# Loading k by head without regrouping, and moving one regrouping of q behind a sum

## The chip, the cores and the metric

One NeuronCore of a Trainium2 chip runs the whole program. The metric is the device time of one execution in microseconds (us), on the slowest core, which here is the only one. A run is compared with runs of the kernel before on the same chip. Runs of the kernel in its undisturbed state are called fast.

## The reference, cut to what matters

Attention without a softmax, a norm per head, then a gated feed-forward layer with a sigmoid-gated residual:

```python
kv  = einsum('bhsd,bhse->bhde', k, v)          # batch 8, heads 8, seq 576, head_dim 64
out = einsum('bhsd,bhde->bhse', q, kv)
x   = out / sqrt(mean(out*out, -1) + 1e-6) * g_norm      # then (4608, 512)
...
ffn = (gelu(x @ w_gate) * (x @ w_val)) @ w_out           # d_ff 1536
y   = x + sigmoid(x @ w_res) * ffn
```

The inputs and outputs are fp32; the kernel works in fp16 with fp32 sums.

## The kernel before

The work goes by blocks of 512 tokens, one for each batch, with the last 64 tokens of every batch gathered in a ninth. While TensorE (PE) does the feed-forward products of block b, the attention of batch b + 1 is slipped in between. The load of a batch brings q and k in by head; VectorE (DVE) regroups both by token. The load of k by head writes the layout `[P, H, NJ*D]`; the regrouped tile has `[P, NJ, H, D]` (P: 128 partitions, H: 8 heads, NJ: 4 tokens in each partition, D: the head's 64 elements).

```python
raw[b, "q"] = stage.tile([P, H, NJ * D], FP16, tag="qraw", name="qraw")
raw[b, "k"] = stage.tile([P, H, NJ * D], FP16, tag="kraw", name="kraw")
nc.gpsimd.dma_start(out=raw[b, "q"], in_=rows4(q, b, 0, H))
nc.gpsimd.dma_start(out=raw[b, "k"], in_=rows4(k, b, 0, H))
...
def by_token(b, which):
    nc.vector.tensor_copy(
        out=b16_t[b, which].rearrange("p j h d -> p h j d"),
        in_=raw[b, which].rearrange("p h (j d) -> p h j d", j=NJ))
...
# a_kv: 32 products per batch read k (8 more read the last tokens)
lhsT=k16[:, j, h, :] if j < NJ else kl[:, h, :]
```

A block ends with its output product, done as seven half-size products over sums of its operands. The order on PE is A, D, A, E, A, F, A; VectorE's sum `wF` has to be done between the second A and the third, because the third overwrites what it reads:

```python
def others():                                            # cut
    prod(w["A"], s_[1], wo_t[:, 1], False)               # PE
    sub(nc.vector, w["F"], w["A"], w["d"], ALU.add)      # VectorE: the sum wF
    prod(w["E"], a_of(blk, 1, 2), b_of(2, 1), False)
    pf((0, 0), w["E"])                                   # VectorE: the gate on wE
    prod(w["A"], s_[2], wo_t[:, 2], False)               # overwrites wA: waits for the sum
    c22 = res_all[part((1, 1))]
    sub(nc.vector, c22, w["A"], w["d"], ALU.add)         # VectorE: the next sum
    prod(w["F"], s_[3], b_of(2, 2), False)
```

The regroupings for batch b are queued on VectorE near the end of block b - 2, so batch 3's stand at the end of block 1, in front of that block's sum wF. Behind q's regrouping SyncE issues the DMA transpose that makes qT.

## Time and profile before

| | |
|---|---|
| time, first three runs | 344.58, 345.43, 344.43 us |
| PE busy | 331.9 us of a 345.4 us span |
| PE's wait on the sum wF, block 1 | 1.2 us, the longest behind the opening |
| regroupings of k on VectorE | 7, mean 738 ns |

The prediction below shows the lines. The rule for reading them: busy shares say which engine is nearest its limit (PE), but what a change gives is decided by PE's waits, each with its releaser, so the list of PE's waits comes first and the order of time around the one wait comes second. In the order of time a line holds the start in us, the duration, the engine, the source line, the operation, output and inputs, the count, and in brackets the idle time before it with its releaser. PEld is PE's loading of weights, ACT is ScalarE, POOL is GpSimd, SPq is SyncE's DMA queue. In a line of the list of waits the numbers are us in total, times, and the longest in us.

### The profile page before, as it was taken

The numbers are of one execution on the slowest core, as the hardware profiler recorded it, in microseconds if no ns is written. First come the engines' busy times: TensorE is split into PE (matmuls) and PEld (weight loads), VectorE is DVE, ScalarE is ACT, GpSimd is POOL, SyncE is SP. The second block draws the span as 40 slices with busy tenths as digits, with TensorE's granted clock in tenths as the row PEclk, the third lists the DMA queues.
The fourth block names the chain that finished last, engine by engine and source line by source line (L and its number), as shares of the span: only waits on it lengthen the run. The fifth ranks groups of instructions, "written<-read, shape, count | busy, mean of one in ns | idle before, by whom it ended". The sixth has DMA issues, their size and how long they took to land.

```text
span 345.4 us, 6165 instructions
## 1 busy us (share of the span) xinstructions
PE 331.9 (96%) x2432; PEld 188.0 (54%) x2432; DVE 236.5 (68%) x446; ACT 150.1 (43%) x265; POOL 103.1 (30%) x121
## 2 busy tenths in 40 slices
PE   8789999999899999999999999999999999999992
PEld 3544454445744475447544764476447644764481
DVE  5665549769859987698578976885688735453643
ACT  3573384274336352535263615361736133623350
POOL 2692161980064108200820083005000600050013
PEclk9899999999999999999999999999999999999997
DMA  7999999669589263966395439744003120030004
GB/s 244 290 178 204 195 204 166 168 95 150 117 108 164 94 123 120 165 60 128 130 167 43 102 114 174 79 92 153 17 0 61 63 76 2 1 121 4 0 2 121
DMA packets 76399, 38.81 MB, mean 112 GB/s; under 512 B 42066, under 2 KB 73810, under 8 KB 76370
## 3 DMA queue, kind: packets, MB, share of 16 engines
q0 software_dynamic: 38752, 17.17, 40.1%
q1 hardware_dynamic: 37184, 20.71, 21.6%
q10 hardware_dynamic: 434, 0.52, 0.5%
q8 instruction: 19, 0.31, 0.4%
q14 instruction: 10, 0.08, 0.1%
HBM read 38.80 MB, written 9.44 MB: 140 GB/s over the span
## 4 chain that ended last, share of the span: by engine, by line
PE 69%; DVE 2%; issue 0%; POOL 0%; POOLq 0%; DVEq 0%
PE gps L336 21%; PE vps L336 20%; PE wA L431 10%; PE rps L356 6%; PE wF L431 3%; PE wD L431 2%; PE w L431 2%; PE wE L431 2%; PE kvp L187 1%; PE op L205 1%; DVE t L282 1%; DVE hid L325 1%; DVE hid_s L404 0%; DVE t L296 0%; POOL osb L526 0%
## 5 line engine op out<-in xcount | busy, mean ns | idle before, releaser
L324 ACT ACTIVATE ge<-gps 128x512 f16<-128x512 f32 x108 | 64.3, 597 | 133.1 <-PE gps L336 127.8
L325 DVE TENSOR_TENSOR hid<-ge,vps 128x512 f16<-128x512 f16 x108 | 73.8, 684 | 63.2 <-PE vps L336 60.8
L336 PE MATMUL vps<-xT,wv 128*128 128x512 f16 x424 | 108.8, 379 | 0.4 <-DVE hid L325 0.4
L336 PE MATMUL gps<-xT,wg 128*128 128x512 f16 x424 | 109.0, 379 | 0.0
L470 POOL TENSOR_TENSOR osb<-osb,t 128x512 f32<-128x512 f32 x28 | 36.1, 1309 | 155.6 <-DVE osb L466 148.6
L336 PEld LDWEIGHTS <-wv 128*128 128x128 f16 x424 | 41.5, 98 | 50.6 <-issue 0.7
L336 PEld LDWEIGHTS <-wg 128*128 128x128 f16 x424 | 40.2, 98 | 45.4 <-issue 0.4
L431 PEld LDWEIGHTS <-hid_s 128*128 128x128 f16 x384 | 37.5, 98 | 6.3 <-issue 1.4
L356 PE MATMUL rps<-wr,xT 128*128 128x512 f16 x144 | 32.7, 379 | 0.0
L431 PEld LDWEIGHTS <-hid 128*128 128x128 f16 x288 | 28.2, 98 | 5.1
L365 ACT ACTIVATE th<-rps 128x512 f32<-128x512 f32 x36 | 21.5, 597 | 19.0 <-PE rps L356 19.0
L356 PEld LDWEIGHTS <-xT 128*128 128x128 f16 x144 | 14.1, 98 | 16.8
L224 DVE TENSOR_REDUCE ss<-sq 128x8 f32<-128x512 f32 x32 | 20.6, 679 | 2.9 <-ACT sq L222 2.7
L431 PE MATMUL wA<-wo_ts,hid_s 128*128 128x256 f16 x168 | 20.6, 273 | 1.2 <-DVE wF L404 1.2
L370 ACT ACTIVATE th<-th 128x512 f32<-128x512 f32 x36 | 19.9, 622 | 0.0
L282 DVE TENSOR_TENSOR t<-op,ny 128x512 f16<-128x512 f32 x28 | 17.9, 682 | 0.1
L222 ACT ACTIVATE sq<-op 128x512 f32<-128x512 f32 x28 | 15.3, 597 | 4.5 <-PE op L205 4.2
L296 DVE TENSOR_TENSOR t<-t,g 128x512 f16<-128x512 f16 x36 | 16.2, 498 | 0.1
L404 DVE TENSOR_TENSOR hid_s<-hid 128x1536 f16<-128x1536 f16 x16 | 15.3, 955 | 0.3
L526 POOL TENSOR_TENSOR osb<-osb,t 128x512 f32<-128x512 f32 (+1 forms) x4 | 4.3, 1078 | 27.8 <-DVE osb L522 27.8
L373 PE MATMUL fps<-wo,hid 128*128 128x512 f16 x48 | 11.2, 379 | 0.0
L431 PE MATMUL wD<-wo_ts,hid_s 128*128 128x256 f16 x84 | 10.3, 273 | 0.1
(133 smaller groups left out, 326.5 us busy)
## 6 DMA issues: line engine op xcount, KB each, us to landing
out_dram<-osb SPq DMA_DIRECT2D x14, 512.0 KB, 2.6
qraw<-in_q_dram POOLq DMA_DIRECT2D x7, 512.0 KB, 8.2
kraw<-in_k_dram POOLq DMA_DIRECT2D x7, 512.0 KB, 9.9
v<-in_v_dram POOLq DMA_DIRECT2D x7, 512.0 KB, 11.9
out_dram<-osb SPq DMA_DIRECT2D x5, 256.0 KB, 2.8
wg<-in_moe_w_gate_dram POOLq DMA_DIRECT2D x2, 512.0 KB, 9.2
wv<-in_moe_w_val_dram POOLq DMA_DIRECT2D x2, 512.0 KB, 9.4
wo<-in_moe_w_out_dram POOLq DMA_DIRECT2D x2, 512.0 KB, 14.2
```

The source lines that it names most:

```text
L222: nc.scalar.activation(out=sq, in_=src, func=AF.Square)
L224: nc.vector.tensor_reduce(out=out_, in_=sq, op=ALU.add, axis=mybir.AxisListType.X)
L282: nc.vector.tensor_tensor(out=t, in0=o, in1=scale, op=ALU.mult)
L296: nc.vector.tensor_tensor(out=t_t[blk][:, jj, :], in0=t_t[blk][:, jj, :], in1=g16, op=ALU.mult)
L324: nc.scalar.activation(out=ge, in_=gps, func=AF.Gelu)
L325: nc.vector.tensor_tensor(out=hids[blk][:, f, :], in0=ge, in1=vps, op=ALU.mult)
L336: nc.tensor.matmul(ps[:, j0 * P : j1 * P], lhsT=w[:, cc, :], rhs=xT_t[blk][:, j0:j1, cc, :], start=(cc == 0 and j0 == 0), stop=(cc == NP - ...
L356: nc.tensor.matmul(rps, lhsT=xT_t[blk][:, j, cc, :], rhs=wr16[:, cc, :], start=(cc == 0), stop=(cc == NP - 1),)
L365: nc.scalar.activation(out=th, in_=rps, func=AF.Tanh, scale=0.5)
L370: nc.scalar.activation(out=th, in_=th, func=AF.Copy, scale=0.5, bias=0.5)
L431: nc.tensor.matmul(ps[:, e - es[0], :], lhsT=a[:, f, e * P : (e + 1) * P], rhs=b[:, f, :], start=(start and e == es[0] and f == 0), stop=( ...
L470: nc.gpsimd.tensor_tensor(out=res_all[of], in0=res_all[of], in1=t_t[blk][of], op=ALU.add)
```

## The change

The intent: let the products read k in the layout in which it is loaded, so that VectorE need not regroup it, and keep batch 3's regrouping of q from standing in front of block 1's sum.

```diff
-        b16_t[b, "k"] = qkvp.tile([P, NJ, H, D], FP16, tag="k16", name="k16")
+        by_head = [P, H, NJ * D] if b > 0 else [P, NJ, H, D]
+        b16_t[b, "k"] = qkvp.tile(by_head, FP16, tag="k16", name="k16")
-        raw[b, "k"] = stage.tile([P, H, NJ * D], FP16, tag="kraw", name="kraw")
-        nc.gpsimd.dma_start(out=raw[b, "k"], in_=rows4(k, b, 0, H))
+        nc.gpsimd.dma_start(out=b16_t[b, "k"], in_=rows4(k, b, 0, H))
...
-                        lhsT=k16[:, j, h, :] if j < NJ else kl[:, h, :],
+                        lhsT=k16[:, h, j * D : (j + 1) * D] if j < NJ else kl[:, h, :],
...
             pf((0, 0), w["E"])
+            for f in rest:
+                f()
             prod(w["A"], s_[2], wo_t[:, 2], False)
...
-            at(m - 1, NF, lambda: by_token(b, "q"))
-            at(m - 1, NF + 1, lambda: by_token(b, "k"), *begin)
+            if b == 3:
+                amid_out[m - 1] = [lambda: by_token(b), *begin]
+            else:
+                at(m - 1, NF, lambda: by_token(b))
+                at(m - 1, NF + 1, *begin)
```

Cut: the staging of the first columns of the value weight, which used k's staging tile and now uses one of k's two tiles, and the places for batches 1 and 2, which lose their k line in the same way.

More of the change, by code (lines that the diff above doesn't have):

```diff
@@ L104, in load_batch, with by_token @@
             load_qr(i)
-    def by_token(b, which):
+    def by_token(b):
         nc.vector.tensor_copy(
-            out=b16_t[b, which].rearrange("p j h d -> p h j d"),
-            in_=raw[b, which].rearrange("p h (j d) -> p h j d", j=NJ),
+            out=b16_t[b, "q"].rearrange("p j h d -> p h j d"),
+            in_=raw[b, "q"].rearrange("p h (j d) -> p h j d", j=NJ),
         )
@@ L438, in prod, with out_by_products @@
                 )
-    def out_by_products(blk, later):
+    def out_by_products(blk, later, rest=()):
         w = {}
@@ L632 @@
     for n, t in (("g", moe_w_gate), ("v", moe_w_val)):
-        r = "q" if n == "g" else "k"
-        w_raw[n] = stage.tile([P, H, NJ * D], FP16, tag=r + "raw", name=f"w{n}f")
+        pool, tag = (stage, "qraw") if n == "g" else (qkvp, "k16")
+        w_raw[n] = pool.tile([P, H, NJ * D], FP16, tag=tag, name=f"w{n}f")
         w_raw[n] = w_raw[n].rearrange("p a b -> p (a b)").bitcast(FP32).rearrange("p (c f) -> p c f", c=NP)
@@ L864, in attn_plan_1 @@
         plan = {
-            NF - 1: [lambda: by_token(b, "q")],
-            NF: [lambda: by_token(b, "k")],
+            NF - 1: [lambda: by_token(b)],
             NF + 3: [
@@ L883 @@
     plans = [{} for _ in range(B + 1)]
+    amid_out = {}
     hold = consts.tile([1, 1], FP16, name="hold")
@@ L905, in plan_attn @@
         if b == 2:
-            at(m, 0, lambda: by_token(b, "q"))
-            at(m, 1, lambda: by_token(b, "k"), *begin)
+            at(m, 0, lambda: by_token(b))
+            at(m, 1, *begin)
             k0, o0, n0 = 4, 6, 9
         else:
-            at(m - 1, NF, lambda: by_token(b, "q"))
-            at(m - 1, NF + 1, lambda: by_token(b, "k"), *begin)
+            if b == 3:
[3 more added lines that the diff above has]
+                at(m - 1, NF + 1, *begin)
             k0, o0, n0 = 1, 3, 7
@@ L955, in products @@
                 s_rest(blk)
-                outs.extend(out_by_products(blk, blk == 1) if blk < B else out_last(blk))
+                outs.extend(out_by_products(blk, blk == 1, amid_out.get(blk, ())) if blk < B else out_last(blk))
             plan.setdefault(NF - 1, []).append(products)
```

## The prediction

> **What bounds the kernel now.** I read the busy row first, then who TensorE (PE) waited for, then VectorE (DVE) and PE in order of time where the one wait lies that the change can touch.
>
> ```profile
> PE 331.9 (96%) x2432; PEld 188.0 (54%) x2432; DVE 236.5 (68%) x446; ACT 150.1 (43%) x265; POOL 103.1 (30%) x121
> ```
>
> PE is busy for 331.9 of 345.4 us. About 13.5 us are all that better feeding could give, and most of that is the opening and the last stores. VectorE at 68% is not the bound as an average, so work taken off it pays only where PE is waiting for it. The list of what PE waited for:
>
> ```profile
> PE kvp L718 <- DVE v L689: 2.5, 2, 2.3
> PE wA L431 <- DVE wF L404: 1.2, 1, 1.2
> ...
> PE vps L336 <- DVE hid L325: 0.4, 1, 0.4
> ```
>
> The first is the opening, before the changed code. The second is one wait of 1.2 us: an output product (wA) waits for a sum on VectorE (wF). The third is a wait for the gated hidden tile. The stretches of 1 us show where the second lies (columns after the stretch: PE, PEld, DVE, ACT, POOL busy, clock, DMA):
>
> ```profile
> 84.00:90.00 6.00, 6.00 (x53) 4.99 (x51) 5.93 (x10) 4.22 (x8) 0.00 (x0) 1.00 0.29 21
> 90.00:91.00 1.00, 0.13 (x2) 0.00 (x0) 1.00 (x3) 0.22 (x1) 0.00 (x0) 1.00 0.27 56
> 91.00:92.00 1.00, 0.65 (x6) 0.58 (x6) 0.89 (x2) 0.00 (x0) 0.00 (x0) 1.00 1.12 214
> ```
>
> PE is full up to 90, then nearly empty for 1.2 us while DVE is full. This is the end of block 1, the products of its output. DVE in order of time there:
>
> ```profile
> 88.06 1.42 DVE L296 TENSOR_TENSOR t<-t,g 128x512 f16<-128x512 f16 x4
> 89.40 0.69 DVE L107 COPY q<-qraw 128x2048 f16<-128x2048 f16 x1
> 90.01 0.69 DVE L107 COPY k<-kraw 128x2048 f16<-128x2048 f16 x1
> 90.61 0.69 DVE L404 TENSOR_TENSOR wF<-wA,wd 128x512 f32<-128x512 f32 x1
> 91.21 0.68 DVE L466 TENSOR_TENSOR osb<-th,wE 128x512 f32<-128x512 f32 x1
> 92.92 0.69 DVE L404 TENSOR_TENSOR osb<-wA,wd 128x512 f32<-128x512 f32 x1 [1.03 <-issue]
> ```
>
> and PE:
>
> ```profile
> 88.66 1.47 PE L431 MATMUL wE<-wo,hid 128*128 128x256 f16 x12
> 91.35 1.47 PE L431 MATMUL wA<-wo_ts,hid_s 128*128 128x256 f16 x12 [1.22 <-DVE wF L404]
> 92.66 1.47 PE L431 MATMUL wF<-wo,hid_s 128*128 128x256 f16 x12
> 93.97 1.47 PE L431 MATMUL wA<-wo_ts,hid 128*128 128x256 f16 x12
> 95.28 1.03 PE L336 MATMUL gps<-xT,wg 128*128 128x512 f16 x4
> ```
>
> The reader is to see that both regroupings of batch 3 (q, then k) stand in VectorE's queue directly ahead of the sum wF, and that PE's next product of wA starts 0.05 us after that sum ends (90.61 + 0.69 = 91.30, then 91.35). VectorE has no idle time in front of the copies: it reaches the sum late because of its queue, not its data. Unhindered, twelve matmuls start 1.31 us apart (92.66 to 93.97), so this product was due at 88.66 + 1.31 = 89.97; PE loses 1.38 us from start to start, recorded as 1.22.
>
> **What the Trainium skill says.** "VectorE: DVE Perf Modes", section "The perf-mode tier table", gives a 16-bit copy of 2048 elements in SBUF 693 ns; the regroupings here take 685 to 687 ns in the median. The same page's section on the errata gives an fp32 tensor_tensor of 512 elements 691 ns; the sums here take 690. So either copy costs the queue what the sum itself costs. "The DRAIN you can't avoid" describes a start-to-start gap after each operation; here starts lie 0.60 to 0.61 us apart, less than the 0.69 us durations, and I count with 0.61. "DMA: Bandwidth & Descriptors", section "Latency and other measured facts", gives DMA transposes 261 GB/s in one kernel; here 214 GB/s moved between 91 and 92 us, so I use the trace's own 4.4 us from issue to landing.
>
> **The change part by part.**
>
> 1. k is loaded straight into the tile that the products read; the regrouping is gone for batches 1 to 7. That takes seven copies off VectorE, 7 x 0.738 = 5.2 us of busy time. PE reads k by columns of 64 elements of one head in either layout, so its 40 instructions per batch stay: no cost, no gain. Six of the seven copies lie where PE has no recorded wait: the copies at 42.73, 63.44 and from batch 4 on. I checked batch 4, the closest call: copies at 125.49 and 126.10, sum at 126.70 ending 127.39, and PE goes on at 127.59 with no idle time. Value of these six: 0. The batch 3 copy, at 90.01, is worth 0.61 us of the sum's start.
>
> 2. Batch 3's regrouping of q goes from before the sum to behind the next operation (the gate that reads wE). That takes a second 0.61 us from ahead of the sum. Together the sum starts at 89.40, where the four scalings of t let go of VectorE, and ends at 90.09; PE goes on at 90.09 + 0.05 = 90.14 in place of 91.35. Gain 1.21 us; 0.17 us of the 1.38 stays, because the scalings are still in front.
>
> 3. What the moved copy costs at its new place. The gate on wE needs that product's end (88.66 + 1.47 = 90.13) and ScalarE's sigmoid (ends 90.22), so it starts near 90.25. The copy follows near 90.85 and ends near 91.55. The next sum waits for PE's wA, started at 90.14: before, it began 92.92 - 91.35 = 1.57 after that start, so it is due at 91.71. The copy fits into idle time that was there already (1.03 us in front of that sum). Cost 0. If it came 0.2 us late, the product that overwrites wA, which is due at 90.14 + 2.62 = 92.76, would still find the sum finished near 92.6.
>
> 4. Buffers. The staged gate weight now borrows one of k's two tiles. k of batch 1 then goes where batch 0's k was; those products start at 17.57 and take 0.4 us, and the load is issued at 22.85. k of batch 2 goes over the staged weight, whose last cast ends near 19.1, and is issued at 43.98. Later loads follow the key-value product of two batches earlier by a whole block. The loads arrive in time: 22.85 + 16.8 (the longest) = 39.7 against a first use at 45.7; 43.98 + 12.7 = 56.7 against 67.4; 73.10 + 8.5 = 81.6 against about 97.6. Cost 0.
>
> Sum: -0.61 - 0.61 + 0 = -1.2 us, 344.58 - 1.2 = 343.4 us, or 0.35%. Everything behind 91 us should shift earlier as a block, since PE is full there.
>
> **The rivals.**
>
> A. The next block's input takes the place of the wait. Block 2's first product reads xT, whose DMA transpose is issued at 89.52, behind the scalings and so not moved by the change:
>
> ```profile
> 89.52 1.78 SPq L313 DMA_TRANSPOSE xT<-t  x1
> 91.46 2.25 SPq L300 DMA_TRANSPOSE qT<-q  x1
> ```
>
> It lands 4.4 us later, at 93.92. PE will want it at 95.28 - 1.21 = 94.07. That leaves 0.15 us, about what passes between a transpose's landing and the instruction that waits for it (qT: 91.46 + 4.3 = 95.76, seen by GpSimd at 95.93). For it: the margin is nothing; against it: it is not negative, and behind it the transposes of q are not earlier than before. I expect 0 to 0.1 us back; a landing 0.5 us later would make it 343.9.
>
> B. The later qT becomes the bound. q is regrouped near 91.55 rather than 90.09, but its transpose had to wait for SyncE's issue of xT until 91.46 anyway, so it starts near 91.65. Landing at 96 and PE's use at 103.5 - 1.2 = 102.3 leave 6 us. GpSimd's loads for batch 4 sit behind it (97.03) and move by 0.2 us; k is due 27 us later. Worth 0.
>
> C. Less VectorE work helps wider, for instance the wait in block 2 for the hidden tile. There PE's starts 116.25 and 117.72 are 1.47 apart in place of 0.86, and wD starts 0.3 late at 123.65. For it: VectorE is full from 111 to 124. Against: no k copy lies there, and the backlog comes from operations that move with PE. If it vanished anyway, the time would be 342.5.
>
> D. The two copies of batch 2 beside GpSimd's sums (1.66 and 1.04 us) show contention. "SBUF - State Buffer", section "Who interferes with whom", says that copies in two-port mode exclude GpSimd for their whole length, and the reverse. Removing one may end GpSimd's sums up to 1 us sooner, but PE waits for neither: VectorE is idle again by 65.1. Worth 0.
>
> **Range and chances.** The three times before spread over 1.0 us, nearly the gain. The size rests on one read interval, so I allow 0.5 us back (A) and as much more (C): 343.4 us, 8 in 10 within 342.7 to 344.2. A change of 2% is 6.9 us, six times the gain and half of all PE idle time: faster 0.01, within 2% 0.98, slower 0.01.
>
> **What would show it.** In the profile after: no copy of k on VectorE after the opening, VectorE busy about 231 us; the sum wF of block 1 directly behind the scalings, ending near 90.1; PE's wait on it 0.2 us or gone; q's copy behind the gate, with little idle time after it; block 2's first gate product near 94.1, not held. It would be wrong if PE waits there for xT (rival A), if the sum is still late because something else slid ahead of it, if a key-value product waits for k's transfer, or if PE's total is shorter elsewhere than at 90 us.

(Where the text says that the staged gate weight borrows k's tile, it is the value weight; the argument about the tile is the same.)

## The result, and the profile after

Ratios are the mean time of one kernel's fast runs over that of the other's fast runs of the same rounds, so they are not quite the ratio of the medians quoted. The square brackets hold a 95% interval. All differences below are under 1%.

| | median | runs | ratio to before |
|---|---|---|---|
| before, at first | 344.50 us | 4 | |
| after, at first | 344.04 us (342.86 to 344.98) | 4 | 0.9981 [0.9956, 1.0006] |
| before, beside e1 to e4 | 344.42 us (344.08 to 344.96) | 11 | |
| after, repeated (e2) | 343.26 us (342.96 to 343.87) | 5 | 0.9973 [0.9960, 0.9986] |

The busy row of the changed kernel:

```profile
PE 330.8 (97%) x2432; PEld 186.8 (55%) x2432; DVE 231.8 (68%) x439; ACT 150.2 (44%) x265; POOL 102.3 (30%) x121
```

VectorE has seven instructions and 4.7 us less; PE has the same instructions. What PE waited for:

```profile
PE kvp L720 <- DVE v L691: 1.4, 1, 1.4
...
PE vps L336 <- DVE hid L325: 0.4, 1, 0.4
```

No wait on wF is left, and the wait in block 2 for the hidden tile is as before. VectorE in order of time at the end of block 1:

```profile
86.51 1.42 DVE L296 TENSOR_TENSOR t<-t,g 128x512 f16<-128x512 f16 x4
87.85 0.69 DVE L404 TENSOR_TENSOR wF<-wA,wd 128x512 f32<-128x512 f32 x1
88.76 0.69 DVE L466 TENSOR_TENSOR osb<-th,wE 128x512 f32<-128x512 f32 x1 [0.22 <-ACT th L370]
89.36 0.69 DVE L107 COPY q<-qraw 128x2048 f16<-128x2048 f16 x1
90.15 0.69 DVE L404 TENSOR_TENSOR osb<-wA,wd 128x512 f32<-128x512 f32 x1
```

and PE:

```profile
87.09 1.47 PE L431 MATMUL wE<-wo,hid 128*128 128x256 f16 x12
88.59 1.47 PE L431 MATMUL wA<-wo_ts,hid_s 128*128 128x256 f16 x12
89.90 1.47 PE L431 MATMUL wF<-wo,hid_s 128*128 128x256 f16 x12
91.21 1.47 PE L431 MATMUL wA<-wo_ts,hid 128*128 128x256 f16 x12
92.52 1.03 PE L336 MATMUL gps<-xT,wg 128*128 128x512 f16 x4
```

The sum stands directly behind the scalings of t, the copy of q behind the gate, and the third A starts 1.50 us after E where it was 2.69 before (88.66 to 91.35). That is 1.19 us. But the two profiled spans differ by 2.8 us (345.4 and 342.6). The other 1.6 us is there before the changed code begins: block 0's first full gate product starts here before,

```profile
23.98 1.03 PE L336 MATMUL gps<-xT,wg 128*128 128x512 f16 x4
```

and here after:

```profile
22.42 1.03 PE L336 MATMUL gps<-xT,wg 128*128 128x512 f16 x4
```

So I measured two distances that leave the opening out. D1 goes from that start to block 2's first gate product; D2 goes from there to the start of the last group of twelve output products. Before: D1 = 95.28 - 23.98 = 71.30 us, D2 = 337.21 - 95.28 = 241.93 us. After: D1 = 92.52 - 22.42 = 70.10 us, D2 = 334.46 - 92.52 = 241.94 us. The change is worth 1.20 us, all of it in D1; nothing is given back later.

### The profile page after: what moved, and what is told of

It reads as the page before. It is cut to its first block, busy times and chain, and to the rows that moved or that the text cites. A ratio compares the mean times of both kernels' runs of the same rounds, so it can differ in the third digit from the quotient of the medians.

```text
span 342.6 us, 6156 instructions
## 1 busy us (share of the span) xinstructions
PE 330.8 (97%) x2432; PEld 186.8 (55%) x2432; DVE 231.8 (68%) x439; ACT 150.2 (44%) x265; POOL 102.3 (30%) x121
## 4 chain that ended last, share of the span: by engine, by line
PE 90%; DVE 4%; DMA 2%; POOL 1%; SPq 1%; issue 1%; POOLq 0%; DVEq 0%
PE gps L336 27%; PE vps L336 26%; PE wA L431 10%; PE rps L356 8%; PE fps L373 3%; PE wD L431 3%; PE wE L431 3%; PE wF L431 3%; PE w L431 2%; DMA kf<-in_k_dram 2%; PE kvp L187 2%; PE op L205 1%; DVE t L282 1%; DVE t L759 1%; DVE hid L325 1%
```

## The experiments

The theory: PE waits in block 1 because two copies stand in VectorE's queue ahead of the sum; each is worth 0.6 us, and the other copies are worth nothing. The rivals: VectorE's total load matters; only one part of the change matters; the opening is changed too; the gain is near a new bound.

**e1, e2: the two kernels once more.** No edit.

> The kernel before, unchanged, timed against itself. My theory: the change is worth 1.2 us at the end of block 1 and the rest of the difference between two runs is made in the first 24 us, where transfers land at varying times. Then this run's ratio is 1.000 with single times about 1 us apart, and its profile has, as before, 71.30 us from block 0's first full gate product (23.98) to block 2's first (95.28), whatever the opening took. Rival (the two kernels' openings differ by something in the change): every run of the kernel before opens late, with its first full gate product near 24.0 us as in the first profile, and none near 22.4.

> The changed kernel, unchanged, for a tighter interval. My theory: 1.2 us of 344.5, a ratio of 0.9965 give or take 0.001, and 70.10 us from block 0's first full gate product to block 2's first, as in its first profile (22.42 to 92.52). Rival (opening differs too): 2.8 us less, ratio 0.992, as the two profiled runs alone would have it. Other rival (the gain is given back later): ratio 0.999 to 1.000.

Measured: e1 344.33 us, ratio 1.0010 [0.9984, 1.0037], five runs at 344.12 to 344.48 and one at 347.46. Its D1 is 71.29 us, but its opening ended at 21.02, 3.0 us earlier than in the first profile of the same kernel.

e2 came to 343.26 us, ratio 0.9973, D1 70.10 us, opening ended at 21.00. So the rival of a changed opening falls: the same program opened at 23.98 and at 21.02, and the two programs at 21.02 and 21.00. The opening is later where the first load of v lands later: its landing took 7.3 us in the first profile of before, 5.4 in e1, 6.3 after, 5.4 in e2 and 7.6 in e3 (opening ended at 25.75). The landing is not all of it. PE's first product of v starts at 10.65 in the first profile of before and at 8.81 in e1, 1.84 us apart; the other 1.1 us came behind it. PE had waited 2.35 us for v there, and the granted clock then fell, which it did not do in e1 (columns: PE, PEld, DVE, ACT, POOL busy, then the clock, DMA share, GB/s):

```profile
11.00:12.00 1.00, 1.00 (x13) 1.00 (x11) 0.29 (x1) 0.59 (x1) 0.27 (x1) 0.50 1.06 367
```

With a spread of this size in the total, four runs could show 0.46 us for a change of 1.2; eleven against five runs show 344.42 - 343.26 = 1.16 us.

**e3: the load of k alone.** q's regrouping stays ahead of the sum.

```diff
-            if b == 3:
+            if b == 99:        # q of batch 3 keeps its old place
                 amid_out[m - 1] = [lambda: by_token(b), *begin]
```

> k is loaded by head without regrouping, but batch 3's regrouping of q stays in front of the sum. My theory: the sum starts one copy (0.61 us) earlier than before, so PE's wait between two products at the end of block 1 goes from 1.38 us (start to start, over 1.31) to 0.77, and the distance from block 0's first full gate product to block 2's first is 70.7 us; ratio 0.998. Rival (only the place of q's copy matters, since the sum waits for the queue to reach it behind q): 71.3 us, ratio 1.000.

Measured: 344.25 us, ratio 1.0010 [0.9975, 1.0045]. One of the six runs, the profiled one, is at 348.29 with a late opening; the others lie at 343.58 to 344.46, so the timing cannot carry a verdict on 0.6 us. The trace can: D1 = 96.45 - 25.75 = 70.70 us, as expected to the last digit, and one copy is left ahead of the sum:

```profile
91.17 0.69 DVE L107 COPY q<-qraw 128x2048 f16<-128x2048 f16 x1
91.78 0.69 DVE L404 TENSOR_TENSOR wF<-wA,wd 128x512 f32<-128x512 f32 x1
```

and PE waits half as long:

```profile
92.53 1.47 PE L431 MATMUL wA<-wo_ts,hid_s 128*128 128x256 f16 x12 [0.63 <-DVE wF L404]
```

**e4: only the places.** k is regrouped as before, but batch 3's two copies both go behind the gate.

```diff
-            at(m - 1, NF, lambda: by_token(b, "q"))
-            at(m - 1, NF + 1, lambda: by_token(b, "k"), *begin)
+            if b == 3:
+                amid_out[m - 1] = [lambda: by_token(b, "q"), lambda: by_token(b, "k"), *begin]
+            else:              # as before
```

> k is still regrouped everywhere, but batch 3's two regroupings both go behind the gate that follows the sum. My theory: the sum starts 1.21 us earlier as in the changed kernel; the two copies take 1.21 us where the changed kernel had room for one, so the next sum begins about 0.5 us late and ends near 1.4 us after the start of the product it reads plus 0.7; the product that overwrites its input, due 2.62 us after that start, waits 0 to 0.3 us. Distance 70.1 to 70.4 us, ratio 0.9965 to 0.9975. Rival (the gain needs k's copy gone, because VectorE is full here): distance 70.7 us or more, ratio 0.998 or above.

Measured: 343.39 us; five of six runs at 343.28 to 343.57, one at 348.04, which pulls the ratio to 0.9992 [0.9954, 1.0029]. D1 is 91.70 - 21.52 = 70.18 us: all but 0.08 us of the gain comes without touching the load of k. The trace shows both copies in the gap and the next sum running straight on:

```profile
88.45 0.69 DVE L107 COPY q<-qraw 128x2048 f16<-128x2048 f16 x1
89.06 0.69 DVE L107 COPY k<-kraw 128x2048 f16<-128x2048 f16 x1
89.66 0.69 DVE L404 TENSOR_TENSOR osb<-wA,wd 128x512 f32<-128x512 f32 x1
```

That sum began 1.98 us after the product it reads (87.68), where it began 1.56 after in the changed kernel (90.15 - 88.59), so it was 0.4 us late. The last A, which overwrites its input, started 1.41 us after F in place of 1.31 (90.40 - 88.99): 0.1 us of the 0.4 reached PE.

**e5: every copy of k but the one that matters.** Batches 1, 2 and 4 to 7 load k by head; batch 3 keeps both copies in place.

```diff
-        by_head = [P, H, NJ * D] if b > 0 else [P, NJ, H, D]
+        by_head = [P, H, NJ * D] if b not in (0, 3) else [P, NJ, H, D]
...
+                at(m - 1, NF, lambda: by_token(b))
+                at(m - 1, NF + 1, lambda: by_token(b, "k"), *begin)     # batch 3
```

> k is loaded by head without regrouping for batches 1, 2 and 4 to 7; batch 3 alone keeps both regroupings in their old place. My theory: the six copies lie where PE waits for nothing, so taking them away gives 0: distance from block 0's first full gate product to block 2's first 71.3 us, ratio 1.000 give or take 0.001. Rival (5.2 us less on VectorE helps wherever it is near full): distance below 71.2 us or less time behind it, ratio 0.998 or below.

Measured: 344.85 us against 344.68 before, five of six runs within 344.61 to 344.89 and one at 348.91; ratio 1.0027 [0.9991, 1.0062]. D1 is 92.79 - 21.50 = 71.29 us and D2 241.94. Six copies fewer on VectorE gave nothing, and PE's wait is the old one:

```profile
PE wA L433 <- DVE wF L406: 1.2, 1, 1.2
```

So it is not VectorE's load.

**e6: one more copy ahead of the sum.** In the kernel before, batch 3's q is regrouped twice (the second writes the same values).

```diff
-            at(m - 1, NF, lambda: by_token(b, "q"))
+            at(m - 1, NF, *[lambda: by_token(b, "q")] * (2 if b == 3 else 1))
```

> The kernel before with batch 3's regrouping of q done twice, one more copy in front of the sum. My theory: the wait grows by one copy's 0.61 us, distance 71.9 us, ratio 1.0017. Rival (the sum's wait has another cause than the copies in the queue ahead of it, for instance PE's own product): distance unchanged at 71.3 us, ratio 1.000.

Measured: 346.22 us, ratio 1.0047 [1.0029, 1.0065]. The direction is the theory's, the size is not: D1 is 95.59 - 21.90 = 73.69 us, 2.39 more than before and not 0.6. PE's lines:

```profile
90.00 1.75 PE L431 MATMUL wA<-wo_ts,hid_s 128*128 128x256 f16 x12 [1.96 <-DVE wF L404]
91.55 2.77 PE L431 MATMUL wF<-wo,hid_s 128*128 128x256 f16 x12
```

The wait grew by 0.74 us, from 1.22 to 1.96: the two copies of q start at 87.32 and k's at 88.65, 1.33 us for two in place of 1.21. The rest is in the products behind the wait: wF's twelve matmuls took 2.77 us, and 1.47 in the kernel before. The stretches of 1 us (PE, PEld, DVE, ACT, POOL busy, then the granted clock, DMA share, GB/s) show why:

```profile
90.00:91.00 1.00, 1.00 (x10) 0.89 (x10) 0.53 (x1) 0.00 (x0) 0.00 (x0) 1.00 1.12 199
91.00:92.00 1.00, 1.00 (x8) 0.71 (x6) 0.15 (x1) 0.00 (x0) 0.00 (x0) 0.52 1.25 272
```

After 1.96 us without work the granted clock fell to 0.50 about 1 us into the next product and stayed there for some 3 us. The six timed runs fall in two groups, 345.35, 345.60 and 345.66 us with a mean clock of 0.997 to 0.998, and 346.78, 347.13 and 347.43 us with 0.991 to 0.992. By these clocks the fall came in three of the six runs; only the profiled one (347.43 us) shows where. A low mean clock alone is no proof of a fall in block 1: the first profile of the kernel before has 0.990 with the fall in its opening, and e1's late run of 347.46 us has 0.990 too.

**e9: two more copies.** The same with three regroupings of q, to see whether a longer wait brings the fall always.

> The kernel before with batch 3's regrouping of q done three times, two more copies in front of the sum. With one more copy PE's wait grew as expected (1.22 to 1.96 us recorded), but in the profiled run and in some of the timed ones the granted clock then fell to 0.50 for some 3 us, and the total grew by 2.4 us in place of 0.7. My theory: it is the length of PE's idle time that brings the fall, and about 2 us is where it begins; with some 2.6 us of idle time every run has it, so all runs lie near 347.8 us (0.6 later than the slower group with one more copy), and the distance from block 0's first full gate product to block 2's first is about 74.3 us. Rival (the fall comes at random, with other causes): some runs still lie near 346.1 us, 1.4 us above the kernel before, with a mean clock of 0.997.

Measured: 347.71 us, ratio 1.0086 [1.0068, 1.0104]; D1 96.05 - 21.62 = 74.43 us, with a wait of 2.69 us. Three of the four runs have a mean clock of 0.990 to 0.992 (347.50, 347.92, 348.16 us), and one has 0.996 (346.58 us). My expectation that every run would have the fall missed: one seems to have escaped it, near what the rival had named (346.1 us, 0.997). What the runs support is that PE's wait of 1.2 us in block 1 brought it in none of the profiles, and that waits of 1.96 and 2.69 us did in the profiled runs and, as the mean clocks suggest, in 3 of 6 and 3 of 4 runs. What decides in a single run stays open.

**e7: the sum ahead of the scalings as well.** The last 0.2 us of the wait can be had by putting the sum first; the scalings of t and the transpose of xT follow it.

```diff
             sub(nc.vector, w["F"], w["A"], w["d"], ALU.add)
+            for f in scal:     # the four scalings of batch 2, then its xT transpose
+                f()
             prod(w["E"], a_of(blk, 1, 2), b_of(2, 1), False)
```

> The changed kernel with the sum put ahead of the four scalings of t too; the scalings and the transpose of xT come right behind the sum. My theory: the sum ends in time for PE (the last 0.2 us of the wait go), but xT's transpose starts about 1.4 us later and lands about 1.3 us after block 2's first gate product is due, so that product waits: distance 71.2 us in place of 70.1, and the wait stands at block 2's first gate product. Rival (there is slack in front of block 2's input): distance 69.9 us, ratio 0.9960 or below.

Measured: 344.91 us against 344.68 before (one of six runs at 349.31); D1 93.28 - 21.82 = 71.46 us, 1.36 more than the changed kernel. The wait on the sum is gone (the third A starts 1.31 us after E in place of 1.50), but the last A comes 0.23 us late behind F (90.65 - 89.11 = 1.54), and block 2's first gate product 1.32 us late behind that A (2.63 in place of 1.31): together 1.36. Block 2 waits for its input. SyncE's line and PE's:

```profile
88.82 1.74 SPq L313 DMA_TRANSPOSE xT<-t  x1
```

```profile
93.28 1.04 PE L336 MATMUL gps<-xT,wg 128*128 128x512 f16 x4 [1.16 <-DMA xT<-t]
```

The transpose took 4.4 us to land, so it landed at 93.22, and PE started 0.06 us later. In the changed kernel it is issued at 87.96 and lands at 92.36; PE starts at 92.52 with no wait. Taking off the same 0.06, its margin is 0.1 us; that D1 grew by 1.36 us when the transpose came 1.46 us later (88.82 - 21.82 against 87.96 - 22.42) says the same. This is the next bound, and it is right behind the gain.

**e8: the wait that is left, in block 2.** The prediction's rival C named it. In block 2 two small operations of batch 3's norm are slow in the changed kernel:

```profile
109.10 0.53 DVE L254 TENSOR_SCALAR nm<-ss 128x40 f32<-128x40 f32 x1
109.66 1.08 DVE L255 TENSOR_SCALAR ny<-nm 128x40 int32<-128x40 int32 x1
```

They run beside GpSimd's additions:

```profile
108.43 2.27 POOL L470 TENSOR_TENSOR osb<-osb,t 128x512 f32<-128x512 f32 x2 [0.36 <-DVE t L296]
```

GpSimd's additions wait for four scalings of block 1's t, which stand in slots 3 to 6 of block 2 (a slot is a place between two groups of the block's feed-forward products). e8 is the changed kernel with those scalings two slots earlier:

```diff
-                    plan.setdefault(3 + j, []).append(g)
+                    plan.setdefault(1 + j, []).append(g)
```

> The changed kernel with block 1's last four scalings of t two slots earlier in block 2, so that GpSimd's additions that follow them are done before VectorE reaches the norm of batch 3. My theory of the wait that is left in block 2 (1.0 us from start to start): two small operations of that norm take 0.53 and 1.08 us beside GpSimd's additions where they take 0.18 each in block 1; with GpSimd done, VectorE's queue is 1.2 us shorter and PE's 0.44 us wait for the hidden tile goes, with the 0.3 us behind it: about 1.0 us less behind block 2's first gate product, ratio near 0.9935 to the kernel before. Rival (the backlog is of VectorE's own work): the norm's operations are short, but PE still waits, or waits elsewhere in block 2, ratio as the changed kernel.

Measured: 342.48 us against 344.68 before, ratio 0.9934 [0.9921, 0.9947]; four fast runs at 342.25 to 342.54, and one of 347.57 us, slow and left out. The same two operations:

```profile
107.96 0.18 DVE L254 TENSOR_SCALAR nm<-ss 128x40 f32<-128x40 f32 x1
108.17 0.18 DVE L255 TENSOR_SCALAR ny<-nm 128x40 int32<-128x40 int32 x1
```

GpSimd's additions now end at 104.47 + 2.27 = 106.74, before them. This agrees with the Trainium skill, "SBUF — State Buffer", section "Who interferes with whom", which counts tensor_scalar among the operations that can contend with GpSimd: 0.53 and 1.08 us beside it, 0.18 without. In the changed kernel the two end at 109.63 and 110.74, each within 0.05 us of the end of one of the additions (109.59 and 110.70). The edit also takes the four scalings out of VectorE's queue ahead of the norm, which could be a cause of its own; but the norm starts 16.58 us after block 2's first gate product in both kernels (109.10 - 92.52, 107.96 - 91.38), so VectorE did not reach it sooner, and some 1.2 us were gained in these two operations. PE's wait for the hidden tile is gone from the list, D1 is 70.09 us as in the changed kernel, and D2 is 240.93 us, 1.01 less. e8 beats the kernel before by 2.2 us. Against the changed kernel it gains 1.0 us in D1 + D2; the two were not timed side by side.

| | D1 us | D2 us |
|---|---|---|
| before; e1 | 71.30; 71.29 | 241.93; 241.94 |
| after; e2 | 70.10; 70.10 | 241.94; 241.94 |
| e3 k's load alone | 70.70 | 241.93 |
| e4 places alone | 70.18 | 241.94 |
| e5 the other copies | 71.29 | 241.94 |
| e6; e9 one, two copies more | 73.69; 74.43 | 241.94; 241.94 |
| e7 sum first | 71.46 | 241.95 |
| e8 GpSimd's additions earlier | 70.09 | 240.93 |

D1 and D2 of either kernel repeated to 0.01 us in its second profile, where single times spread over 1 us and more.

## Why the prediction was right

It said 343.4 us; the two sets of runs have medians of 344.04 and 343.26 us, and the mechanism's own size, 1.21 us predicted, is 1.20 us in D1.

1. *k's copy of batch 3 is worth 0.61 us, the other six nothing.* Right: 0.60 in e3, 0.01 in e5. (VectorE's busy time fell by 4.7 us and not by the 5.2 of seven whole copies.)
2. *q's move is worth another 0.61, and 0.17 of the wait stays.* Right: from e3 to the changed kernel D1 falls by 0.60, and the third A starts 1.50 us after E, 0.19 above the 1.31 of an unhindered one.
3. *The moved copy fits its new place.* Right: from the start of wF on, the gate was put at 0.85, the copy at 1.45 and the next sum at 2.31 us; measured are 0.91, 1.51 and 2.30. It is a close fit: e4's second copy no longer fits it.
4. *No buffer makes anything wait.* Right: no product of k waits for k's transfer, and D2 is unchanged.
5. *Rival A, xT in place of the sum: 0 to 0.1 us back.* The wait did not come: D1 lost nothing. The margin of 0.15 us was real, and e7 shows it by using it up. The prediction thought that about all of it passes between landing and use, a reading taken from GpSimd; PE took 0.06 us, so 0.1 us is left.
6. *Rival B, the later qT.* It started at 90.20, right behind q's copy, and no product waited for it.
7. *Rival C, the wait in block 2.* Right that no copy of k has to do with it: it is still 0.44 us. The prediction called the backlog one of "operations that move with PE"; e8 shows that GpSimd's additions beside it were part of the cause. The size that the prediction gave it, 343.4 - 342.5 = 0.9 us, was about right: e8 took off 1.0.
8. *Rival D, GpSimd's sums.* Nothing in D1 or D2 moved but the sum's wait, so it was worth nothing. GpSimd's six sums beside the copy did shorten, from 7.61 to 7.16 us.

What the prediction left out is where the times scatter. It read a spread of 1.0 us off three runs, but not where it is made. In the profiles it is made in the opening, where it can exceed the gain (D2 is the same in all but e8); the single late runs of e1, e4, e5 and e7 have no profile, so their place is not shown. The first comparison showed 0.46 us, less than the gain, with an interval that includes no gain, and by itself it would not have settled that there is one. The range of 342.7 to 344.2 us was built from rivals A and C, neither of which moved the time; that it held the first median of 344.04, by 0.16 us, is partly luck.

## What to carry to other kernels

Before taking work off an engine that is not the bound, find the one place where the bounding engine waits for it, and count the instructions that stand in the queue in front of the awaited one: here two copies of 0.61 us gave 1.20 us, six like them gave nothing, and moving both gave nearly as much (1.12) as removing one and moving the other. Look then for what is due next behind the gain (here a transpose with 0.1 us to spare), and measure an effect of this size between two marks in the trace, since the scatter of the opening hides it in the total.

## What the Trainium skill lacked or had wrong

- "TensorE: Matmul & The Clock Gate", section "Part 1: The HAM clock gate", puts the half-rate state after at least one idle window of about 3.4 us, and its section "HAM oscillation" gives the rule "no PE-idle gaps >~3.4µs". Here shorter gaps sufficed: after 1.96 us of idle time the granted clock was 0.50 for some 3 us (e6; 3 of 6 runs by their mean clock), after 2.69 us likewise (e9; 3 of 4 runs), after 2.35 us in the opening of the kernel before, and after the 1.2 us of block 1 in no profile. In e3's opening five warm-up matmuls behind a wait of 1.61 us took 2.34 us in place of 1.24, though the clock column showed 1.00 there. The page says that the window runs freely, which would fit a fall in some runs only; no run here shows that this is the reason.
- "VectorE: DVE Perf Modes", section "The DRAIN you can't avoid", calls a DRAIN of roughly the operation's duration less 266 ns a start-to-start gap; taken so, that would be about 0.42 us for an operation of 0.69 us (an estimate from the page's figure). The distance of two starts that counts for a queue was larger here: copies and sums recorded at 0.69 us start 0.60 to 0.61 us apart, and one copy taken out ahead of PE's wait gave 0.60 us (e3).
- No page that I read gives the spread of a load's landing time: the first load of v took 5.4 to 7.6 us from issue to landing in eleven profiles, and the opening ended between 21.00 and 25.75 us.
